# Linear attention times a gated SwiGLU block on one core: a fifth product of the last stage goes to a second Strassen level, and its preparation is moved between engines

## The chip, the cores and the metric

The kernel runs on one core of a Trainium2 chip. The metric is the device time of one execution in microseconds (us); the time before is the median of three runs. PE is the matrix engine TensorE, DVE is VectorE, ACT is ScalarE, POOL is GpSimd, and SP is SyncE, which only issues transfers here. Each engine works through its own queue of instructions in order, and waits at one until the semaphores that it names have come.

## The reference, cut to what matters

```python
xn  = layernorm(x)                       # x: [1, 2048, 1024] bf16
s   = linear_attention(xn, wqkv, wo)     # 32 heads of 32
g   = silu((silu(xn @ w_gate) * (xn @ w_up)) @ w_down)   # F = 3584
out = x + s * g
```

The change touches the product with `w_down` for the second half of the tokens, what prepares its weights, and the loads of `x` and `s` for the last line.

## The kernel before

The 2048 tokens are handled in two passes of 1024. A pass has a gate/up stage (28 weight groups, the products at line 966) that leaves `h`, transposed, in SBUF, and a down stage that multiplies `h` by `w_down`. All large products use the seven-product Strassen-Winograd scheme instead of eight. The first pass ends in `emit_down`, the second in `emit_down_m`.

**The first down stage** (`emit_down`). It goes over token tiles t of 128 in two phases: phase a (four products per k) for tiles 0, 1, then 2, 3; phase b (three products per k) for tiles 2, 3 (`hf == 1`) and then 0, 1 (`hf == 0`). The two tiles of a half are staggered by `LEAD` = 6 of the 14 steps `st`. The sums `dzw` take two of the eight PSUM banks that the pools share out for each tile, and there are two such buffers. So in phase b tile 0 takes over the buffer of tile 2, and tile 1 that of tile 3, once `evac_b` has read them (the VectorE addition `dd`, line 1294, is the first instruction in it on that engine). VectorE, ScalarE and TensorE run in program order here; the `w_down` tiles of phase b are the seven `(p, "b", j)` tiles.

**The second level.** In the last pass seven products M1 to M7 are made one after another, M_ORDER = 1, 2, 7, 6, 5, 4, 3. A product in `L2` is itself split into seven half-width products (`l2_M`, matmuls of 256 columns at line 1466); the others are 56 matmuls of 512 columns (`prod_t`, line 1430). A second-level product needs sums of its weights, four subtractions for each pair j of weight rows, stored to DRAM (`l2_drams`) and loaded again, and sums of its left side (`l2_lhs`). The weight sums come in two ways:

- `l2_early` makes them from the phase b tiles of the first down stage while those lie in SBUF: the subtractions are at line 1132, on GpSimd, and three transfers on SyncE's queue store them (lines 1124 to 1126). The four results T go to the free fourth part of the tile itself. Before, this is done for M2.
- `l2_load` and `l2_sums` load the weights again in the second gate/up stage, into a weight slot, make the sums on GpSimd (line 1144) and store them from its queue (line 1145). Before, this is done for M1 and M4.

**Weight slots.** One pool of eight 1 MB slots (`w_slot`) serves every weight tile. `load_w_to(n)` asks for the tiles up to the n-th of a fixed list `w_seq`; a load waits on SyncE's queue until a slot is free. `r_spare` is a pair of slots that is later used for M1's left-side sums; `x_spare` is a pair of spare tiles for those of M2 and M4.

**The output.** `fin` multiplies by `s` and adds `x` (lines 1200, 1201, VectorE), stores the tile (line 1202), and calls `io_load`, which loads `x` and `s` for a later output tile (lines 1191, 1192, SyncE) into one of five `io` buffers. The last three tiles of the kernel have buffers of their own, in the space of the finished sums S0, S1 and S2:

```python
pool, tg = (sp, "S%d" % len(fq)) if len(fq) < 3 else (iop, "io")
```

In `emit_down_m` the sums kept over the products are KA and KB. M5 gives the block c22 (`tt(c, M5[t], KB[t])`, then silu and `fin`, tile by tile while M5 runs), and M3 is accumulated in PSUM on top of M5 (`out3`, `prod_t(3, t, M5[t], False)`). GpSimd makes M4's left-side sums (lines 1163 to 1166). The functions the diff touches:

Of the kernel before, what the change touches and what calls it, by code (L numbers as in the profile page):

```python
# [10 lines left out]
ALU = mybir.AluOpType  # L11
# [10 lines left out]
def kernel(  # L22
# [165 lines left out]
    passes = list(range(NPASS - 1, -1, -1))  # L188
    NWA = NFG // 2
    M_ORDER = (1, 2, 7, 6, 5, 4, 3)  # L190
    L2 = (1, 2, 4)
    L2_ORDER = (1, 2, 5, 6, 7, 4, 3)
    NQ = NFG // 2
    CH = CW // 2
# [757 lines left out]
    with ExitStack() as p3:  # L952
# [143 lines left out]
            eng.tensor_tensor(out=a21.bitcast(F16), in0=a12, in1=S2, op=ALU.subtract)  # L1096
            s_ring[(hf, m)] = (S1, S2, S3)

        l2_q = deque((M, j) for M in L2 if M != 2 for j in range(0, NQ, 2))
        l2_live = deque()  # L1100

        def l2_load():
            M, j0 = l2_q.popleft()
            kd, q = M_PACK[M]
            t = w_slot()
            v = t[:].rearrange("p h a b -> p (h a b)").rearrange("p (b j n) -> p b j n", b=8, n=CH)
            js = range(j0, min(j0 + 2, NQ))
            for j in js:
                for k, b0, b1 in ((0, 0, 7), (1, 1, 6)):
                    src = wd_drams[j][0 if kd == "a" else 1][:, k, q].rearrange("p (c n) -> p c n", n=CH)  # L1110
                    nc.sync.dma_start(out=v[:, b0:b1 + 1:b1 - b0, j - j0, :], in_=src)
            l2_live.append((M, js, v))

        def l2_early(M, j, store):

            t = w_tiles[(passes[0], "b", j)][:].rearrange("p h a b -> p (h a b)")
            q = M_PACK[M][1]
            w = t[:, 0:6 * CW].rearrange("p (k q c n) -> p q k c n", k=2, q=3, c=2)[:, q]
            T = t[:, 6 * CW:8 * CW].rearrange("p (b n) -> p b n", b=4)
            if store:  # L1120
                if M not in l2_drams:
                    l2_drams[M] = dram.tile([P, 7, NQ, CH], BF16, name="l2_%d" % M)
                d = l2_drams[M]
                nc.sync.dma_start(out=d[:, 0:2, j], in_=w[:, :, 0])
                nc.sync.dma_start(out=d[:, 6, j], in_=w[:, 1, 1])
                nc.sync.dma_start(out=d[:, 2:6, j], in_=T)
                return
            r = w.bitcast(F16) if M >= 4 else w
            t1, t2, t3, t4 = [T[:, i].bitcast(F16) for i in range(4)]
            for o_, a_, b_ in ((t1, r[:, 0, 1], r[:, 0, 0]), (t2, r[:, 1, 1], t1), (t3, r[:, 1, 1], r[:, 0, 1]),  # L1130
                               (t4, r[:, 1, 0], t2)):
                nc.gpsimd.tensor_tensor(out=o_, in0=a_, in1=b_, op=ALU.subtract)

        def l2_sums():
            M, js, v = l2_live.popleft()
# [11 lines left out]
        x_spare, r_spare = [], []  # L1147

        def l2_bufs(M):
            v = [x[:].rearrange("p a b -> p (a b)").bitcast(F16) for x in x_spare]  # L1150
            if M == 1:
                v = [x[:].rearrange("p h a b -> p (h a b)").bitcast(F16) for x in r_spare]
            v = [x[:, 0:2 * NQ * 2 * P].rearrange("p (s j r n) -> p s j r n", s=2, j=NQ, r=2) for x in v]
            return [v[0][:, 0], v[0][:, 1], v[1][:, 0], v[1][:, 1]]

        def l2_quad(A, j):
            v = A[:, :, j].rearrange("p k (r t n) -> p k r t n", r=2, t=2)
            return v[:, 0, :, 0], v[:, 1, :, 0], v[:, 0, :, 1], v[:, 1, :, 1]

        def l2_lhs(M, A, j, eng):  # L1160
            a11, a12, a21, a22 = l2_quad(A, j)
# [22 lines left out]
        def io_load(after=None):  # L1184
            if not fq:
                return
            p, t, cc = key = fq.pop(0)
            r0 = p * TB2 + t * P
            pool, tg = (sp, "S%d" % len(fq)) if len(fq) < 3 else (iop, "io")
            io = pool.tile([P, 2, CW], BF16, name="io", tag=tg)  # L1190
            gate([nc.sync.dma_start(out=io[:, 0, :], in_=x2[r0:r0 + P, cc * CW:(cc + 1) * CW]),
                  nc.sync.dma_start(out=io[:, 1, :], in_=s_dram[r0:r0 + P, cc * CW:(cc + 1) * CW])],
                 after, sync=True)
            io_tiles[key] = io

# [10 lines left out]
        def emit_down(p, h, base, last, more_S, next_S):  # L1206
# [152 lines left out]
            for hf in (1, 0):  # L1359
                t0, t1 = 2 * hf, 2 * hf + 1  # L1360
                fresh = hf == 0
                endz = last and fresh
                for st in range(NFG if endz else NS):
                    if st == 4:
                        while pend:
                            pend.pop(0)()
                    if hf == 1 and not last and st % 2 == 1 and 2 in L2:
                        if st // 2 < NQ:
                            l2_early(2, st // 2, False)
                        if 0 <= st // 2 - 2 < NQ:  # L1370
                            l2_early(2, st // 2 - 2, True)
                    if st < NFG:
                        step_b(t0, st, fresh)
                        if st == NFG - 1:
                            fins = evac_b(t0, fresh)
                    if st >= LEAD and not endz:
                        step_b(t1, st - LEAD, fresh)
                        if fresh and (st - LEAD) % 2 == 1:
                            load_w_to(base + 2 * NWA + (st - LEAD) // 2 + 2)
                if endz:  # L1380
                    for f in fins:
                        f()
                    finish(t1)
                    break
                fins2 = evac_b(t1, fresh)
                for f in fins:
                    f()
                if fresh:
                    deferred.extend(fins2)
                else:  # L1390
                    for f in fins2:
                        f()

        def emit_down_m(p, h, base):
# [8 lines left out]
            def load(M, q=None):  # L1403

                n_ = max(i for i, key in enumerate(seq) if key[2][0] == M and q in (None, key[2][1])) + 1
                load_w_to(base + n_ + (NPK - 2 if M == 1 and q != 3 else NPK))

            def S3(k):
                return s3_[k // NWA][:, k % NWA]
# [59 lines left out]
            def l2_M(M, A, K, done, fill, in_place, dst=None):  # L1469
# [24 lines left out]
                for r in range(2):  # L1494
                    c0, c1 = c[r]
                    if K is None:
                        nc.scalar.copy(out=c1[:, hi], in_=zy[r][:, lo])
                        nc.scalar.copy(out=c0[:, hi], in_=zy[r][:, hi])
                        nc.scalar.copy(out=c0[:, lo], in_=xw[r][:, lo])
                    else:  # L1500
                        tt(c1[:, hi], zy[r][:, lo], K[2 * r + 1][:, hi])
                        tt(K[2 * r][:, hi] if in_place else c0[:, hi], zy[r][:, hi], K[2 * r][:, hi])
# [1 line left out]
                            tt(c0[:, lo], xw[r][:, lo], K[2 * r][:, lo])  # L1504
                    tt(c1[:, hi], xw[r][:, hi], c1[:, hi])
                fill()
                for r in range(2):
                    l2_p(M, 4, r, A, bk)
                load(M, 2)
                for r in range(2):  # L1510
# [2 lines left out]
                        nc.scalar.copy(out=c1[:, lo], in_=zy[r][:, lo])  # L1513
                    else:
                        tt(c1[:, lo], zy[r][:, lo], K[2 * r + 1][:, lo])
                        done(2 * r + 1, c1)
                    l2_p(M, 3, r, A, bk)
                    if in_place:
# [18 lines left out]
            load_w_to(base + NPK - 2)  # L1537
            KA = kept("kA")
            fins = deque()
            M7, M6, M5 = [], [], []  # L1540
            KB = []

            def fill7():
# [17 lines left out]
                flush(1)  # L1561
            load(7)
            sums(S4, A12, S2, ALU.subtract)
            for j in range(NQ):
                l2_lhs(4, quads(h, 1, 1), j, nc.gpsimd)
            M6 = banks()
            for t in range(TPB):
                prod_t(6, t, M6[t], True)
                tt(KB[t], M6[t], KB[t])
                tt(KA[t], M6[t], KA[t])  # L1570
            load(6)
            M5 = banks()
            for t in range(TPB):
                prod_t(5, t, M5[t], True)
                c = k2([P, CW], FP32, "c22")[:]
                tt(c, M5[t], KB[t])
                fins.append((t + TPB, 1, silu(c, "g22")))
                if len(fins) > 1:
                    flush(1)
            tt(KA[-1], M5[-1], KA[-1])  # L1580
            load(5)

            def out3(t):
                prod_t(3, t, M5[t], False)
                c = k2([P, CW], FP32, "c12")[:]
                tt(c, M5[t], KA[t])
                fins.append((t, 1, silu(c, "g12")))

            def done4(t, c):
                fins.append((t + TPB, 0, silu(c, "g21")))  # L1590

            def fill3():
# [21 lines left out]
        for pi, p in enumerate(passes):  # L1614
# [69 lines left out]

            na0 = 6 if first else 8
            l2_j = 0
            load_w_to(base + na0)
            if first:
                wd_pipe2(-1)
# [3 lines left out]
            for i in range(n):  # L1693
# [38 lines left out]
                if not first:  # L1732
                    if l2_live:
                        l2_sums()
                    if i in (17, 18):
                        r_spare.append(w_slot())
                    if i % 2 == 1 and l2_q:
                        l2_load()
                    if i >= 18 and 4 * l2_j + 4 <= i:
                        l2_lhs(1, quads(h, 0, 0), l2_j, nc.gpsimd)  # L1740
                        l2_lhs(2, quads(h, 1, 0), l2_j, nc.gpsimd)
                        l2_j += 1
                if deferred:
                    deferred.pop(0)()
            base += n
            if last_pass:
                l2_lhs(2, quads(h, 1, 0), NQ - 1, nc.gpsimd)
# [36 lines left out]
```

## Time and profile before

| | |
|---|---|
| median of 3 runs | 755.94 us (755.38 to 756.78) |
| profiled execution: its time, its span | 756.18 us, 754.4 us |
| PE busy, share of the span | 745.8 us, 99% |
| DVE / ACT / POOL busy | 581.4 / 381.1 / 399.8 us |
| granted PE clock, mean | 0.999 |
| second pass: gate/up, products | about 498.5 to 668.9 us, 668.9 us to the end |

The page of a profile gives busy times by engine, a chain of work that ended last, and groups of instructions by line. The trace behind it can be asked for the instructions of one engine in order of time: start, duration, engine, line, and in brackets how long the engine stood still just before and what ended that. "SPq" is SyncE's queue, and its lines are the issues of transfers; a transfer "lands" when its data is there. PE is at work for 99% of the span, so a moment in which it stands still is a moment of the total.

### The profile page before, as it was taken

The page shows a single profiled execution, that of the slowest core. Times are in us where ns is not written, and L with a number is a line of the kernel's source. Part 1 is how long each engine was busy: PE and PEld are TensorE (multiplying, and loading weights), DVE is VectorE, ACT ScalarE, POOL GpSimd, SP SyncE. Part 2 cuts the span into 40 slices and gives each one's busy share as a digit, 9 for nine tenths or more (in the row PEclk, how much of TensorE's full clock was granted, in tenths as well). Part 3 has the DMA queues.
Part 4 walks back from the last instruction along what each step waited for, and adds up shares of the span by engine and source line. Part 5 has one row for each costly group of instructions (what it writes and reads, how often), then busy time and mean ns, then how long its engine had stood idle before and what let it go on. Part 6 is the DMA issues. An engine that isn't in the chain of part 4 may idle for free.

```text
span 754.4 us, 11075 instructions
## 1 busy us (share of the span) xinstructions
PE 745.8 (99%) x3857; PEld 360.8 (48%) x3857; DVE 581.4 (77%) x1040; ACT 381.1 (51%) x545; POOL 399.8 (53%) x500
## 2 busy tenths in 40 slices
PE   8999999999999999999999999999999999999997
PEld 3544444454454444444444444444444444467464
DVE  6687787887697788888889785468776877687966
ACT  5677776889956575656658311132323222232023
POOL 2444799998540266868585021811542569434900
PEclk9999999999999999999999999999999999999999
DMA  9967799879779668878799228789786768479652
GB/s 318 304 146 139 228 332 298 303 158 271 206 190 296 231 214 301 295 279 316 273 323 409 111 65 306 222 295 339 258 306 222 281 206 344 147 258 318 209 161 77
DMA packets 129160, 187.77 MB, mean 249 GB/s; under 512 B 36208, under 2 KB 104176, under 8 KB 119376
## 3 DMA queue, kind: packets, MB, share of 16 engines
q1 hardware_dynamic: 121760, 156.00, 63.9%
q0 software_dynamic: 5904, 28.58, 9.9%
q10 hardware_dynamic: 1440, 2.49, 1.1%
q8 instruction: 30, 0.49, 0.3%
q14 instruction: 26, 0.21, 0.1%
HBM read 119.47 MB, written 60.23 MB: 238 GB/s over the span
## 4 chain that ended last, share of the span: by engine, by line
PE 84%; DMA 7%; POOL 3%; DVE 2%; issue 2%; ACT 1%; SPq 1%; POOLq 0%; DVEq 0%; ACTq 0%
PE zw L966 19%; PE kv_ps L554 15%; PE xb L966 10%; PE q_ps L183 6%; PE dzw L1228 6%; PE dm L1430 6%; PE yb L966 5%; PE dm L1466 4%; PE dx L1228 3%; DMA l<-w_sb 3%; PE fx L816 3%; DMA w_sb<-wd 3%; PE s_ps L774 3%; POOL w_sb L1144 2%; PE dy L1228 2%
## 5 line engine op out<-in xcount | busy, mean ns | idle before, releaser
L966 PEld LDWEIGHTS <-w_sb 128*128 128x128 f16 (+1 forms) x1568 | 152.1, 98 | 183.8 <-DMA w_sb<-pk_u 1.3
L966 PE MATMUL xb<-xnT,w_sb 128*128 128x512 bf16 x448 | 115.0, 379 | 0.0
L554 PE MATMUL kv_ps<-wkv_sb,xnT 128*128 128x512 bf16 x512 | 113.7, 379 | 0.6 <-ACT xnT L543 0.4
L966 PE MATMUL zw<-xnT,w_sb 128*128 128x512 bf16 x448 | 105.8, 379 | 0.0
L966 PE MATMUL zw<-S,w_sb 128*128 128x512 f16 x448 | 105.8, 379 | 0.0
L321 POOL TENSOR_TENSOR w_sb<-w_sb 128x512 f16<-128x512 bf16 x42 | 50.2, 1195 | 95.7 <-DVE w_sb L309 51.3
L286 ACT ACTIVATE w_sb<-w_sb 128x2048 bf16<-128x2048 bf16 x42 | 79.9, 1902 | 3.9 <-DMA w_sb<-in_B_w_up_dram 3.9
L554 PEld LDWEIGHTS <-xnT 128*128 128x128 bf16 x512 | 48.3, 97 | 56.0 <-ACT xnT L543 0.8
L1144 POOL TENSOR_TENSOR w_sb<-w_sb 128x512 f16<-128x512 bf16 (+3 forms) x32 | 35.4, 1126 | 52.4 <-DMA w_sb<-wd 51.9
L1042 ACT ACTIVATE sg<-cg 128x1024 bf16<-128x1024 f32 x28 | 29.6, 1057 | 57.4 <-DVE cg L1035 57.4
L183 PE MATMUL q_ps<-xnT,wq_sb 128*128 128x512 bf16 x256 | 58.4, 379 | 0.0
L966 PE MATMUL yb<-S,w_sb 128*128 128x512 f16 x224 | 57.4, 379 | 0.8 <-DMA w_sb<-pk_u 0.8
L1035 DVE SCALAR_TENSOR_TENSOR cg<-zw,rc_all,s 128x1024 f32<-128x1024 f32 x28 | 35.9, 1284 | 25.3 <-PE zw L966 13.2
L994 DVE SCALAR_TENSOR_TENSOR s<-yb,rc_all,s 128x512 f32<-128x512 f32 x42 | 31.5, 749 | 27.3 <-ACT s L993 27.3
L322 POOL TENSOR_TENSOR w_sb<-w_sb 128x512 f16<-128x512 bf16 x42 | 50.5, 1202 | 3.3
L324 POOL TENSOR_TENSOR w_sb<-w_sb 128x512 f16<-128x512 bf16 x42 | 50.3, 1197 | 0.0
L323 POOL TENSOR_TENSOR w_sb<-w_sb 128x512 f16<-128x512 bf16 x42 | 50.2, 1196 | 0.0
L1202 POOL DMA_DIRECT2D out_dram<-io x16 | 8.9, 555 | 69.2 <-DVE io L1201 69.0
L993 ACT ACTIVATE s<-xb,rcl 128x512 f32<-128x512 f32 x14 | 9.6, 687 | 66.3 <-PE xb L966 66.3
L1228 PE MATMUL dx<-w_sb,hT 128*128 128x512 bf16 x112 | 42.4, 379 | 0.0
L993 ACT ACTIVATE s<-xb,rc_all 128x512 f32<-128x512 f32 x42 | 28.4, 676 | 22.0 <-issue 12.7
L309 DVE TENSOR_SCALAR w_sb<-w_sb,cs_all 128x2048 bf16<-128x2048 bf16 x35 | 36.7, 1048 | 2.8
(213 smaller groups left out, 1351.1 us busy)
## 6 DMA issues: line engine op xcount, KB each, us to landing
w_sb<-pk_g SPq DMA_DIRECT2D x27, 1024.0 KB, 6.6
pk_g<-w_sb SPq DMA_DIRECT2D x14, 1024.0 KB, 5.0
w_sb<-pk_u SPq DMA_DIRECT2D x14, 1024.0 KB, 8.3
pk_u<-w_sb POOLq DMA_DIRECT2D x13, 1024.0 KB, 5.8
w_sb<-l SPq DMA_DIRECT2D x9, 896.0 KB, 4.6
w_sb<-in_B_w_gate_dram SPq DMA_DIRECT2D x14, 512.0 KB, 6.4
w_sb<-in_B_w_down_dram SPq DMA_DIRECT2D x28, 256.0 KB, 4.8
w_sb<-in_B_w_up_dram SPq DMA_DIRECT2D x14, 512.0 KB, 5.4
```

Of the source, the lines that this page charges most:

```text
L183: nc.tensor.matmul(q_ps[:], lhsT=wq_sb[:, dc, g * P:(g + 1) * P], rhs=xn_ap(dc, btok), start=(dc == 0), stop=(dc == DC - 1))
L286: nc.scalar.activation(out=junk, in_=raw_view(key, t), func=ACT.Square, accum_out=asum[:])
L321: nc.gpsimd.tensor_tensor(out=T1, in0=b12, in1=b11, op=ALU.subtract)
L322: nc.gpsimd.tensor_tensor(out=T2, in0=b22, in1=T1, op=ALU.subtract)
L323: nc.gpsimd.tensor_tensor(out=T3, in0=b22, in1=b12, op=ALU.subtract)
L324: nc.gpsimd.tensor_tensor(out=T4, in0=b21, in1=T2, op=ALU.subtract)
L554: mm = nc.tensor.matmul(kv_ps[:], lhsT=xn_ap(dc, tok), rhs=wkv_sb[:, dc, c * CW:(c + 1) * CW], start=(dc == 0), stop=(dc == DC - 1))
L966: mm = nc.tensor.matmul(out, lhsT=lhs(k), rhs=rhs(k), start=(first and k == 0), stop=(k == HK - 1), skip_group_check=True)
L993: nc.scalar.activation(out=s1[:], in_=x_[:], func=ACT.Copy, scale=rc)
L1144: nc.gpsimd.tensor_tensor(out=b(o_), in0=b(a_), in1=b(b_), op=ALU.subtract)
L1228: nc.tensor.matmul(out, lhsT=lhs, rhs=rhs, start=first, stop=lastk, skip_group_check=True)
L1430: nc.tensor.matmul(out, lhsT=lhs_of(M)(k)[:, t * P:(t + 1) * P], rhs=w_of(M, k)[:, cols], start=first and k == 0, stop=k == NFG - 1, skip_ ...
```

## The change

- `L2` becomes (1, 2, 4, 5): M5 is made of seven half-width products. Its result is collected in a new tile pair `T5`, in the space S0, S1; `done5` then adds it to KA and KB. c22 is finished (`silu`, `fin`) only in `fill3`, inside M4. M3 starts fresh in its own banks. The first two half products of M4 are made inside M5, as those of M2 are inside M1.
- The weight sums of M2 **and M4** are now made in `l2_early`, on VectorE, in phase b of the first down stage: M2's for tile j at step st = 3 + j, M4's at st = 10 + j, all in `hf == 1`; their stores three and two steps later on SyncE's queue.
- In the second gate/up stage M1 and M5 are loaded again, through two slots that are held for it (`r_spare`) from i = 3 until M5 is done; the prefetch in the last stage is two tiles shorter for that. GpSimd's left-side sums of M2 are spread from i = 4 on.
- The left-side sums of M5 and M4 are made on VectorE by `l2_lhs_all`, eight larger instructions each.
- All residual tiles go through the five `io` buffers. SyncE's queue is in program order in the second gate/up stage.

```diff
-    L2 = (1, 2, 4)
+    L2 = (1, 2, 4, 5)
+    L2_EARLY = (2, 4)
...
         def l2_load():
...
-            t = w_slot()
+            while len(r_spare) < 2:
+                r_spare.append(w_slot())
+            t = r_spare[len(l2_q) % 2]
...
-                nc.gpsimd.tensor_tensor(out=o_, in0=a_, in1=b_, op=ALU.subtract)
+                nc.vector.tensor_tensor(out=o_, in0=a_, in1=b_, op=ALU.subtract)
...
+        def l2_lhs_all(M, A, eng):
+            sb = l2_bufs(M)
+            for r in range(2):
+                v = A.rearrange("p k j (r t n) -> p k j r t n", r=2, t=2)[:, :, :, r]
+                a11, a12, a21, a22 = v[:, 0, :, 0], v[:, 1, :, 0], v[:, 0, :, 1], v[:, 1, :, 1]
+                s1, s2, s3, s4 = [x[:, :, r] for x in sb]
+                eng.tensor_tensor(out=s1, in0=a21, in1=a22, op=ALU.add)
+                eng.tensor_tensor(out=s2, in0=s1, in1=a11, op=ALU.subtract)
+                eng.tensor_tensor(out=s3, in0=a11, in1=a21, op=ALU.subtract)
+                eng.tensor_tensor(out=s4, in0=a12, in1=s2, op=ALU.subtract)
...
         def io_load(after=None):
-            pool, tg = (sp, "S%d" % len(fq)) if len(fq) < 3 else (iop, "io")
+            pool, tg = iop, "io"
...
         def emit_down(p, h, base, last, more_S, next_S):
-                    if hf == 1 and not last and st % 2 == 1 and 2 in L2:
-                        if st // 2 < NQ:
-                            l2_early(2, st // 2, False)
-                        if 0 <= st // 2 - 2 < NQ:
-                            l2_early(2, st // 2 - 2, True)
+                    if not last:
+                        for M, q0, dq, lag in zip(L2_EARLY, (3, 10), (1, 1), (3, 2)):
+                            for d, store in ((0, False), (lag, True)):
+                                j, rem = divmod(st + (1 - hf) * NS - q0 - d, dq)
+                                if rem == 0 and 0 <= j < NQ:
+                                    l2_early(M, j, store)
...
         def emit_down_m(p, h, base):
-                load_w_to(base + n_ + (NPK - 2 if M == 1 and q != 3 else NPK))
+                load_w_to(base + n_ + (NPK - 2 if M in (1, 2, 7, 6, 5) and (M, q) != (5, 3) else NPK))
...
-            for j in range(NQ):
-                l2_lhs(4, quads(h, 1, 1), j, nc.gpsimd)
+            l2_lhs_all(5, quads(h, 0, 1).bitcast(F16), nc.vector)
...
-            M5 = banks()
-            for t in range(TPB):
-                prod_t(5, t, M5[t], True)
-                c = k2([P, CW], FP32, "c22")[:]
-                tt(c, M5[t], KB[t])
-                fins.append((t + TPB, 1, silu(c, "g22")))
-                if len(fins) > 1:
-                    flush(1)
-            tt(KA[-1], M5[-1], KA[-1])
-            load(5)
+            l2_lhs_all(4, quads(h, 1, 1), nc.vector)
+            T5 = [sp.tile([P, 2, CW], FP32, name="kT", tag="S%d" % r) for r in range(2)]
+            T5 = [T5[t // 2][:, t % 2] for t in range(TPB)]
...
+            def done5(t, T):
+                tt(KA[t], T, KA[t])
+                tt(T, T, KB[t])
...
             def fill3():
+                for t in range(TPB):
+                    fins.append((t + TPB, 1, silu(T5[t], "g22")))
                 flush()
+                M3.extend(banks())
                 out3(0)
-            go(l2_M(4, quads(h, 1, 1), KB, done4, fill3, True))
+            m4_ = l2_M(4, quads(h, 1, 1), KB, done4, fill3, True)
+            go(l2_M(5, quads(h, 0, 1).bitcast(F16), None, done5, lambda: next(m4_), False, T5))
+            go(m4_)
...
+            if last_pass:
+                sp_man.enter_context(tc.manual_schedule(engines={mybir.EngineType.SP}))
...
-                    if i in (17, 18):
-                        r_spare.append(w_slot())
-                    if i % 2 == 1 and l2_q:
+                    if i >= 3 and i % 2 == 1 and l2_q:
                         l2_load()
```

More of the change, by code (lines that the diff above doesn't have):

```diff
@@ L1097, in emit_hs @@
             s_ring[(hf, m)] = (S1, S2, S3)
-        l2_q = deque((M, j) for M in L2 if M != 2 for j in range(0, NQ, 2))
+        l2_q = deque((M, j) for M in L2 if M not in L2_EARLY for j in range(0, NQ, 2))
         l2_live = deque()
+        x_spare, r_spare = [], []
         def l2_load():
@@ L1145, in l2_sums @@
             nc.gpsimd.dma_start(out=l2_drams[M][:, :, js.start:js.stop, :], in_=v[:, 0:7, 0:n_, :])
-        x_spare, r_spare = [], []
         def l2_bufs(M):
             v = [x[:].rearrange("p a b -> p (a b)").bitcast(F16) for x in x_spare]
-            if M == 1:
+            if M in (1, 5):
                 v = [x[:].rearrange("p h a b -> p (h a b)").bitcast(F16) for x in r_spare]
@@ L1188, in io_load @@
             r0 = p * TB2 + t * P
-            pool, tg = (sp, "S%d" % len(fq)) if len(fq) < 3 else (iop, "io")
+            pool, tg = iop, "io"
             io = pool.tile([P, 2, CW], BF16, name="io", tag=tg)
-            gate([nc.sync.dma_start(out=io[:, 0, :], in_=x2[r0:r0 + P, cc * CW:(cc + 1) * CW]),
-                  nc.sync.dma_start(out=io[:, 1, :], in_=s_dram[r0:r0 + P, cc * CW:(cc + 1) * CW])],
+            eng = nc.sync
+            gate([eng.dma_start(out=io[:, 0, :], in_=x2[r0:r0 + P, cc * CW:(cc + 1) * CW]),
+                  eng.dma_start(out=io[:, 1, :], in_=s_dram[r0:r0 + P, cc * CW:(cc + 1) * CW])],
                  after, sync=True)
@@ L1497, in l2_M @@
                         nc.scalar.copy(out=c1[:, hi], in_=zy[r][:, lo])
-                        nc.scalar.copy(out=c0[:, hi], in_=zy[r][:, hi])
-                        nc.scalar.copy(out=c0[:, lo], in_=xw[r][:, lo])
                     else:
@@ L1506, in l2_M @@
                 fill()
+                if K is None:
+                    for r in range(2):
+                        nc.scalar.copy(out=c[r][0][:, hi], in_=zy[r][:, hi])
+                        nc.scalar.copy(out=c[r][0][:, lo], in_=xw[r][:, lo])
                 for r in range(2):
@@ L1515, in l2_M @@
                         tt(c1[:, lo], zy[r][:, lo], K[2 * r + 1][:, lo])
+                    if done is not None:
                         done(2 * r + 1, c1)
@@ L1539, in emit_down_m @@
             fins = deque()
-            M7, M6, M5 = [], [], []
+            M7 = []
             KB = []
@@ L1571, in emit_down_m @@
             load(6)
-            M5 = banks()
-            for t in range(TPB):
-                prod_t(5, t, M5[t], True)
-                c = k2([P, CW], FP32, "c22")[:]
-                tt(c, M5[t], KB[t])
-                fins.append((t + TPB, 1, silu(c, "g22")))
-                if len(fins) > 1:
-                    flush(1)
-            tt(KA[-1], M5[-1], KA[-1])
-            load(5)
+            l2_lhs_all(4, quads(h, 1, 1), nc.vector)
+            T5 = [sp.tile([P, 2, CW], FP32, name="kT", tag="S%d" % r) for r in range(2)]
+            T5 = [T5[t // 2][:, t % 2] for t in range(TPB)]
             def out3(t):
-                prod_t(3, t, M5[t], False)
+                prod_t(3, t, M3[t], True)
                 c = k2([P, CW], FP32, "c12")[:]
-                tt(c, M5[t], KA[t])
+                tt(c, M3[t], KA[t])
                 fins.append((t, 1, silu(c, "g12")))
@@ L1590, in done4 @@
                 fins.append((t + TPB, 0, silu(c, "g21")))
+            def done5(t, T):
+                tt(KA[t], T, KA[t])
+                tt(T, T, KB[t])
+            M3 = []
             def fill3():
+                for t in range(TPB):
+                    fins.append((t + TPB, 1, silu(T5[t], "g22")))
                 flush()
+                M3.extend(banks())
                 out3(0)
-            go(l2_M(4, quads(h, 1, 1), KB, done4, fill3, True))
+            m4_ = l2_M(4, quads(h, 1, 1), KB, done4, fill3, True)
+            go(l2_M(5, quads(h, 0, 1).bitcast(F16), None, done5, lambda: next(m4_), False, T5))
+            go(m4_)
             hs_ = [slice(0, 3 * CW // 4), slice(3 * CW // 4, CW)]
@@ L1686 @@
             l2_j = 0
+            sp_man = ExitStack()
+            if last_pass:
+                sp_man.enter_context(tc.manual_schedule(engines={mybir.EngineType.SP}))
             load_w_to(base + na0)
@@ L1734 @@
                         l2_sums()
-                    if i in (17, 18):
-                        r_spare.append(w_slot())
-                    if i % 2 == 1 and l2_q:
+                    if i >= 3 and i % 2 == 1 and l2_q:
                         l2_load()
-                    if i >= 18 and 4 * l2_j + 4 <= i:
+                    if i >= 19 and 4 * l2_j + 4 <= i:
                         l2_lhs(1, quads(h, 0, 0), l2_j, nc.gpsimd)
-                        l2_lhs(2, quads(h, 1, 0), l2_j, nc.gpsimd)
                         l2_j += 1
+                    if i % 4 == 0 and i >= 4:
+                        l2_lhs(2, quads(h, 1, 0), i // 4 - 1, nc.gpsimd)
                 if deferred:
                     deferred.pop(0)()
+            sp_man.close()
             base += n
```

## The prediction, made before the changed kernel had run

> **What bounds the kernel now.** The page first: TensorE works in 99% of the span, so it is the bound in every stage.
>
> ```profile
> PE 745.8 (99%) x3857; PEld 360.8 (48%) x3857; DVE 581.4 (77%) x1040; ACT 381.1 (51%) x545; POOL 399.8 (53%) x500
> ```
>
> A change can win in two ways only: fewer matmuls, or less of the few microseconds in which TensorE stands still. It loses wherever it makes TensorE wait. The chain that ended last gives the pace of the two kinds of product, and TensorE's timeline the two waits that the changed places hold today:
>
> ```profile
> 734.62 3.02 PE dm L1430 x14
> 737.64 3.06 PE dm L1466 x28
> 623.81 1.04 PE L966 MATMUL yb<-S,w_sb 128*128 128x512 f16 x4 [0.82 <-DMA w_sb<-pk_u]
> 728.35 1.69 PE L1466 MATMUL dm<-w_sb,hT 128*128 128x256 f16 x14 [0.28 <-ACT dm L1478]
> ```
>
> A 512-column matmul takes 3.02 / 14 = 0.2157 us, a 256-column one 3.06 / 28 = 0.1093 us. Next, what VectorE does when the first down stage changes from tiles 2, 3 to tiles 0, 1 (timelines of VectorE, then of TensorE):
>
> ```profile
> 448.97 0.42 DVE L1093 TENSOR_TENSOR S<-hT 128x512 f16<-128x512 bf16 x1
> 449.42 0.42 DVE L1094 TENSOR_TENSOR S<-S,hT 128x512 f16<-128x512 f16 x1
> 449.76 0.42 DVE L1095 TENSOR_TENSOR S<-hT 128x512 f16<-128x512 bf16 x1
> 450.22 0.42 DVE L1096 TENSOR_TENSOR hT<-hT,S 128x512 f16<-128x512 bf16 x1
> ...
> 468.10 1.23 DVE L714 TENSOR_TENSOR xnT<-xnT,S 128x2048 f16<-128x2048 bf16 x1
> 469.24 0.42 DVE L1200 TENSOR_TENSOR g<-g,io 128x512 bf16<-128x512 bf16 x1
> ...
> 476.05 1.22 DVE L1294 TENSOR_TENSOR dd<-dzw,s 128x1024 f32<-128x1024 f32 x1 [5.14 <-PE dzw L1228]
> 480.58 1.23 DVE L1294 TENSOR_TENSOR dd<-dzw,s 128x1024 f32<-128x1024 f32 x1 [3.31 <-PE dzw L1228]
> ```
> ```profile
> 480.60 0.59 PE L1228 MATMUL dzw<-w_sb,hT 128*128 128x512 f16 x2
> ...
> 484.48 0.59 PE L1228 MATMUL dzw<-w_sb,hT 128*128 128x512 f16 x2
> ```
>
> VectorE stands idle 5.14 us before the first `dd` (tile 2) and 3.31 us before the second (tile 3). TensorE takes those two buffers again at 480.60 and 484.48, so the first `dd`, over at 477.3, has 3.3 us to spare. Last, the tail on VectorE and SyncE:
>
> ```profile
> 750.75 0.35 DVE L1200 TENSOR_TENSOR g<-g,io 128x384 bf16<-128x384 bf16 x1
> 751.13 0.36 DVE L1201 TENSOR_TENSOR io<-g,io 128x384 bf16<-128x384 bf16 x1
> 751.41 0.22 DVE L1200 TENSOR_TENSOR g<-g,io 128x128 bf16<-128x128 bf16 x1
> ```
> ```profile
> 736.86 0.34 SPq L1202 DMA_DIRECT2D out_dram<-io  x1
> 738.58 0.33 SPq L1191 DMA_DIRECT2D io<-in_A_x_dram  x1
> 738.96 1.00 SPq L1192 DMA_DIRECT2D io<-s_dram  x1
> ```
>
> A residual load waits until the store from its buffer has landed: here 1.7 us, in other pairs of this stretch up to 2.6.
>
> **Part 1, the weight sums on VectorE.** GpSimd loses 28 subtractions of 0.705 us (19 us); VectorE gets 56 of 128x256. The trace has no such two-byte row on VectorE; the sizes around it are 128x128 (0.22 us) and 128x384 (0.35), so I take 0.285. Starts lie the duration plus 0.03 apart where one needs the result before it, and the duration less 0.07 where not (0.45 and 0.34 for the 0.42 us rows above). Four for one pair j make 2 x 0.315 + 2 x 0.21 = 1.05 us.
>
> In the changed kernel's instruction order, eleven of the fourteen groups (M2's seven, M4's first four) stand **ahead of** the first `dd`, and three between it and the second. Ahead of them is the same work as before, to 469.24, and two `fin` (1.58 us). So the first `dd` starts at 469.24 + 1.58 + 11 x 1.05 = 482.4 and ends at 483.6: TensorE waits 3.0 us. The second ends at 483.6 + 3 x 1.05 + 1.22 = 488.0; TensorE, now 3.0 late, wants it at 487.5: 0.5 more. **Cost 3.5 us**; nothing hides it, as TensorE has no gap before the end. If the sums ran at the 128x128 rows (0.80 a group), the cost would be 0.2; at the 128x384 rows (1.32), 7.2. The true size lies midway, so I keep 3.5 and both ends for the range.
>
> M4's sums overwrite the T area of M2's, so each also waits for M2's store on SyncE. The stores stand behind the first gate tile's load, which landed at 475.8 before; its tiles can be asked for earlier now, as SyncE no longer waits 25.6 us for GpSimd's first sums. Uncovered, this adds up to 2 us. Behind the stores are 10 residual loads and the load of the first up tile, issued at 494.32 before and wanted about 7.5 us later; I get 496.3, against a TensorE that is 3.5 us late. Cost nothing, by about 2 us.
>
> The granted clock was 1.00 throughout the down stage and 0.91 only in the last 10.4 us, where TensorE idled 4.6. The Trainium skill ("TensorE: Matmul & The Clock Gate", Part 1) says that an idle window of some 3.4 us halves the clock until TensorE has again been busy for as long. By it a 3.0 us wait is just spared, and a longer one could cost some 1.7 us more, an estimate from that page.
>
> **Part 2, M5.** It goes from 56 x 0.2157 = 12.08 us to 98 x 0.1093 = 10.71: **1.4 us gained**, and the 0.28 wait at M4's start goes too, as ScalarE no longer has a c22 silu in front of that copy. VectorE gets 16 left-side sums of 896 columns (about 0.6 each, between the 512 and 2048 rows above: 9.5 us) and some 3.7 us more of additions, but GpSimd's 28 sums (29 us) leave, beside which VectorE's 128x1024 sums took 1.06 instead of some 0.7. I get M6's additions done by 718, and M4 takes those banks at 722. Cost nothing; with that 4 us cover gone, microsecond for microsecond.
>
> The prefetch is two tiles shorter in M1 and M2: M7's first tile is asked for at 679.4 (when M2's first tile is free) instead of 675.4, and is wanted from 687.1 on; it landed in 5.5. Cost nothing, up to 1.5.
>
> **Part 3, the second gate/up stage.** SyncE's queue waited 47 us for stores of the slots that the sums passed through; with two slots of their own the 0.82 us wait should go: **0.8 gained**. Next late would be the sums themselves (load, sums, store: about 19 us of a 24 us cycle). A loss of the same size bounds it on the other side.
>
> **Part 4, the residual tiles.** Four c22 `fin`, formerly 3 us apart within M5, now come together when M4's fifth half product is done (732.7): VectorE ends them at 734.8, 735.6, 736.4, 737.2. SyncE's order is then store, store, store, load, load, load, store, load (each load a pair), each load behind the landing of an earlier store (1.9 us): the fourth store goes out at 739.5, its load at 741.4, and it lands (2.3 us) at 744.1. That tile is for the first `fin` after M3's second tile, where VectorE would be at 742.5. The last three tiles have lost their own buffers and come behind the stores of that same run: the last lands at 751.5, and the final `fin` ends at 752.6 instead of 751.9. So the end is 0.7 later, although TensorE ends 1.7 earlier. With landings of 2.6 us it is 1.7 later, without any wait 1.7 earlier. I take **1.2 later, M5's gain used up in it**.
>
> **The sum**: 3.5 - 0.8 + 1.2 = 3.9. The profiled execution took 756.18 us (span 754.4); 756.18 + 3.9 = 760.1. It lay 0.24 above the median, so 759.8.
>
> **The rivals.** (a) *Faster*: the sums cost VectorE little enough that the buffer is free in time. The first `dd` must end by 480.6, so eleven groups have 8.55 us, 0.78 each; and the tail must not wait. Then 755.9 - 0.8 - 1.7 = 753.4. For: VectorE is idle for 8.4 us there. Against: even the half-size row gives 0.80. (b) *Only the stall*: the residual tiles come in time; 755.9 + 3.5 - 0.8 - 1.7 = 756.9. For: stores can land in 1.7. Against: SyncE's order of stores and loads. (c) *Heavier*: M4's sums wait for the stores, the clock drops or M7's weights are late; 2 to 5 us on top, 762 to 765. For: the first gate tile took 12.9 us to land. Against: less is queued beside it now.
>
> **How the numbers follow.** About 0.2% (1.5 us) can be told from no change. Forecast 0.50, heavier 0.24, both slower; (b) 0.12, counted as the same; (a) 0.14. The range reaches from 755.0, below (b) and above (a), to 764.5, the upper end of the sums plus a late tail.
>
> **What would show it.** TensorE idle about 3 us ahead of the `dzw` matmul of tile 0 at 480.6, released by VectorE's `dd`, which comes after eleven groups of some 1.05 us; no idle time before the first of the two `dd`; no wait near 620; M5 with 98 matmuls of 0.109; VectorE waiting for an `io` load between 742 and 751 of the old time. The prediction is wrong if `dd` still starts at 476, or if TensorE takes other banks first.

## The result and the profile after

The changed kernel takes 762.54 us (median of 9 runs) against 756.65 us of the kernel before on the same chip: ratio 1.0073, interval 1.0057 to 1.0089, so slower, as forecast: 5.9 us more by these medians, where 3.9 more were forecast (759.8, range 755.0 to 764.5, from a median before of 755.94). The profiled execution took 762.54 us, its span is 760.8 us, 6.4 more than before. The page's busy times:

```profile
PE 741.0 (97%) x3835; PEld 365.0 (48%) x3899; DVE 592.1 (78%) x1119; ACT 385.2 (51%) x557; POOL 356.4 (47%) x444
```

TensorE's share fell from 99% to 97%: what was lost, it lost standing still. (Some 64 of its matmuls are missing from this record, so its busy time is a little low; it has 42 more to do than before, 98 of M5 for 56.) Its timeline shows two waits, in the first down stage and just behind it:

```profile
482.94 0.59 PE L1242 MATMUL dzw<-w_sb,hT 128*128 128x512 f16 x2 [1.79 <-DVE dd L1308]
...
512.08 1.04 PE L967 MATMUL yb<-S,w_sb 128*128 128x512 f16 x4 [1.54 <-DMA w_sb<-pk_g]
```

The first was forecast, at 3.0 + 0.5 us. VectorE's timeline (line 1136 are the weight sums, 1308 is the `dd`) shows why it is shorter, and a later wait of VectorE for a residual load, at 496.74:

```profile
472.33 9.41 DVE L1136 TENSOR_TENSOR w_sb<-w_sb 128x256 f16<-128x256 bf16 x40
481.66 1.22 DVE L1308 TENSOR_TENSOR dd<-dzw,s 128x1024 f32<-128x1024 f32 x1
482.80 2.88 DVE L1136 TENSOR_TENSOR w_sb<-w_sb 128x256 f16<-128x256 f16 x12
485.59 1.22 DVE L1308 TENSOR_TENSOR dd<-dzw,s 128x1024 f32<-128x1024 f32 x1
...
496.74 0.43 DVE L1214 TENSOR_TENSOR g<-g,io 128x512 bf16<-128x512 bf16 x1 [5.95 <-DMA io<-s_dram]
```

Ten groups pass in 9.33 us, 0.93 each; VectorE does not stand still before `dd`, and the second `dd` is in time. The wait at 496.74 is not new, but in the kernel before it ended 3.8 us earlier:

```profile
492.98 0.42 DVE L1200 TENSOR_TENSOR g<-g,io 128x512 bf16<-128x512 bf16 x1 [5.10 <-DMA io<-s_dram]
```

The second wait of TensorE, for a gate tile, was not in the sum. SyncE's timeline shows what stood ahead of that tile:

```profile
490.75 0.83 SPq L1130 DMA_DIRECT2D l<-w_sb  x1
491.69 0.67 SPq L1205 DMA_DIRECT2D io<-in_A_x_dram  x1
...
497.88 0.38 SPq L264 DMA_DIRECT2D w_sb<-pk_u  x1
504.48 0.33 SPq L1205 DMA_DIRECT2D io<-in_A_x_dram  x1
...
505.40 0.39 SPq L264 DMA_DIRECT2D w_sb<-pk_g  x1
```

and in the kernel before:

```profile
488.33 0.35 SPq L1191 DMA_DIRECT2D io<-in_A_x_dram  x1
...
494.32 0.38 SPq L263 DMA_DIRECT2D w_sb<-pk_u  x1
...
499.83 0.38 SPq L263 DMA_DIRECT2D w_sb<-pk_g  x1
```

The gate tile stands behind one residual load, which waits until an output tile has left its buffer: VectorE's `fin` at 496.74, its store from GpSimd's queue at 497.92, landed at 504.4, 6.5 us later. Before, the same store took from 494.16 to 498.9. So the gate tile is asked for 5.6 us later than before, while TensorE is only 2.3 us later. Of the 5.6, 3.8 come from the later `fin`, whose own residual load went out at 491.69 instead of 488.33 (SyncE comes to it straight from the last of M4's stores; but the output tile whose buffer it takes was itself stored only at 487.89 instead of 485.50); the other 1.8 come from the slower landing of the store. The table by stretches of 5 us shows what else is new there (columns: stretch, length, busy time of PE, PEld, DVE, ACT and POOL with counts, granted clock, busy share of the DMA engines, GB/s). Two stretches of the kernel before:

```profile
485.00:490.00 5.00, 5.00 (x25) 2.27 (x24) 2.78 (x7) 0.00 (x0) 3.21 (x6) 1.00 0.60 184
495.00:500.00 5.00, 5.00 (x25) 2.23 (x23) 2.29 (x4) 1.76 (x2) 0.00 (x0) 1.00 0.77 265
```

and the same of the changed kernel:

```profile
485.00:490.00 5.00, 4.95 (x24) 2.25 (x23) 4.86 (x13) 1.15 (x1) 1.60 (x3) 1.00 1.00 279
495.00:500.00 5.00, 5.00 (x25) 2.27 (x24) 2.58 (x4) 1.21 (x2) 0.54 (x1) 1.00 1.00 254
```

With M4's 3 MB of stores the DMA engines are full from 475 to 500. Last, the tail, on VectorE and on SyncE:

```profile
748.28 0.43 DVE L1214 TENSOR_TENSOR g<-g,io 128x512 bf16<-128x512 bf16 x1 [2.51 <-DMA io<-s_dram]
...
753.92 0.43 DVE L1214 TENSOR_TENSOR g<-g,io 128x512 bf16<-128x512 bf16 x1 [0.97 <-DMA io<-s_dram]
```
```profile
738.57 1.92 SPq L1216 DMA_DIRECT2D out_dram<-io  x3
...
743.41 0.42 SPq L1216 DMA_DIRECT2D out_dram<-io  x1
745.72 0.33 SPq L1205 DMA_DIRECT2D io<-in_A_x_dram  x1
```

TensorE's last matmul ends at 751.05; VectorE's last `fin` at 757.85, 6.8 us behind it. Before it was 2.1 (749.80 and 751.89).

**The 6.4 us, read from the two traces**: 0.57 had passed before the changed place (I don't count it to the change: in the other runs' profiles VectorE reached the same instruction there 0.8 us earlier to 0.6 us later than before); + 1.79 for `dd`; + 1.54 for the gate tile; − 0.82, the wait near 620, which is gone; − 1.82 from M6's first matmul to M3's second tile (38.33 us before, 36.51 after); + 4.71, the tail of VectorE behind TensorE; + 0.4 behind the last `fin`.

### The profile page after: what moved, and what is told of

Same layout as the page of the kernel before. It is cut to its first block, busy times and chain, and to the rows that moved or that the text cites. A ratio compares the mean times of both kernels' runs of the same rounds, so it can differ in the third digit from the quotient of the medians.

```text
span 760.8 us, 11165 instructions
## 1 busy us (share of the span) xinstructions
PE 741.0 (97%) x3835; PEld 365.0 (48%) x3899; DVE 592.1 (78%) x1119; ACT 385.2 (51%) x557; POOL 356.4 (47%) x444
## 4 chain that ended last, share of the span: by engine, by line
PE 88%; DVE 5%; DMA 4%; issue 1%; ACT 1%; SPq 0%; DVEq 0%; ACTq 0%
PE zw L967 25%; PE kv_ps L555 14%; PE xb L967 12%; PE q_ps L183 6%; PE yb L967 6%; PE dzw L1242 5%; PE dm L1481 4%; PE dm L1445 3%; PE fx L817 3%; PE s_ps L775 2%; PE dx L1242 2%; PE dy L1242 2%; DVE w_sb L1136 1%; PE kvz L577 1%; PE nd L744 1%
## 5 line engine op out<-in xcount | busy, mean ns | idle before, releaser
L967 PE MATMUL xb<-xnT,w_sb 128*128 128x512 bf16 x420 | 113.3, 379 | 1.5
```

The costliest lines, as they stand in the source:

```text
L967: mm = nc.tensor.matmul(out, lhsT=lhs(k), rhs=rhs(k), start=(first and k == 0), stop=(k == HK - 1), skip_group_check=True)
```

## Experiments

All were compared with the kernel before on their own chip. One thousandth in a ratio is 0.76 us. The changed kernel stands at 1.0073.

**The buffers of the last tiles.** Edit:

```diff
-            pool, tg = iop, "io"
+            pool, tg = (sp, "S%d" % len(fq)) if len(fq) < 3 else (iop, "io")
...
-            T5 = [sp.tile([P, 2, CW], FP32, name="kT", tag="S%d" % r) for r in range(2)]
-            T5 = [T5[t // 2][:, t % 2] for t in range(TPB)]
+            T5 = xnp.tile([P, TPB, CW], FP32, name="kT", tag="xn8")
+            T5 = [T5[:, t] for t in range(TPB)]
```

> The changed kernel with one thing undone: the last three residual tiles have buffers of their own again (M5's T tiles take another tile instead). Theory A (the tail is late because those tiles wait for the stores of the same run): the waits of 2.5, 1.0 and 0.8 us on VectorE after 748 go, the last fin ends some 2.1 us after TensorE's last matmul as it did in the kernel before, instead of 6.8: 4.7 us less, 757.8. Rival B (the tail is late because the four c22 fin come together and the stores with them, whatever buffers the last tiles have): the waits stay, 762.5 within 1 us.

Measured: 761.21 us, ratio 1.0039 (1.0023 to 1.0056). The waits behind 752 are gone, but VectorE still waits 3.02 us at 748.8, and its last `fin` ends 5.2 us behind TensorE. By the ratios it is 2.6 us less than the changed kernel, where theory A had 4.7. So both theories were half right: the buffers are 1.6 of the 4.7 us of the tail in the profile, and something else is 3.1.

The same cause alone, in the kernel before (only the first pair of lines above, the other way round):

> The kernel before with that one thing alone: all residual tiles pass through the five io buffers. Theory A (the buffers are enough to make the tail late): 3 to 5 us slower than before, 759.5 to 761.5. Rival B (it takes the bunched c22 fin as well, here they lie 3 us apart): at most 1 us slower, 756.5 to 757.5.

Measured: 759.32 us, ratio 1.0017 (0.9999 to 1.0036), between the two and just not clear of no change. In the profile the last `fin` ends 4.3 us behind TensorE, 2.2 more than before: the buffers cost about that on their own, without any bunching.

**The order in which the tiles are loaded.** The first `fin` after M3's second tile is that of c12's first tile; in the list of loads this tile stands behind the four of c21, so it is the fourth of the loads that follow the c22 stores. Edit, with own buffers:

```diff
-                fq += [(p, t + dt, cc) for dt, cc in ((0, 0), (TPB, 1), (TPB, 0), (0, 1)) for t in range(TPB)]
+                fq += [(p, t + dt, cc) for dt, cc in ((0, 0), (TPB, 1)) for t in range(TPB)]
+                fq += [(p, 0, 1)] + [(p, t + TPB, 0) for t in range(TPB)] + [(p, t, 1) for t in range(1, TPB)]
```

> The changed kernel with own buffers for the last three residual tiles, and with the residual loads of the last pass in the order in which the fin take them (the first c12 tile ahead of the four c21 tiles instead of behind them). Theory A (VectorE's wait of 2.5 to 3.0 us at 748 arises because the first fin after M3's second tile takes the tile that was asked for last): that tile is asked for long before, the wait shrinks to the 0.5 us or less that the last of the four loads is late for its own fin, and the last fin ends some 2.1 us after TensorE: 2.5 less than with own buffers alone, 758.5 against 761.2. Rival B (the wait is passed on to the next fin, whose loads are as late): less than 1 us, 760.5 or more.

Measured: 758.96 us, ratio 1.0012 (1.0001 to 1.0023). Theory A. VectorE's timeline has one wait for a transfer left in the tail:

```profile
747.99 0.43 DVE L1215 TENSOR_TENSOR g<-g,io 128x512 bf16<-128x512 bf16 x1 [0.51 <-DMA io<-s_dram]
```

The last `fin` ends 2.7 us behind TensorE. SyncE's queue is what it was (the fourth store at 742.7, its load at 745.2): that load is as late as ever, but now it belongs to the fourth `fin` after M3's second tile, not to the first.

This run's profile also shows, unasked, what a slightly longer wait does:

```profile
482.32 0.89 PE L1243 MATMUL dzw<-w_sb,hT 128*128 128x512 f16 x2 [2.23 <-DVE dd L1309]
483.00 0.63 PE L1243 MATMUL dx<-w_sb,hT 128*128 128x512 bf16 x1
```

A `dx` matmul is shown with 0.63 instead of 0.38, and the granted clock of 480 to 485 is 0.75. Three groups of three matmuls (two `dzw`, one `dx`) take 3.63 us, from 482.32 to 485.95, instead of 1.94: 1.7 us on top of the wait.

**The work ahead of `dd`.** The four 128x2048 sums of the next pass stand ahead of the weight sums on VectorE (4.9 us). Edit:

```diff
             if not last:
                 emit_rcl()
-                emit_Ssum(passes[passes.index(p) + 1])
...
                 fins2 = evac_b(t1, fresh)
+                if not last and not fresh:
+                    emit_Ssum(passes[passes.index(p) + 1])
```

> The changed kernel with the four 128x2048 sums of the next pass (4.9 us on VectorE) moved behind the last of the down stage's dd. Theory A (the first dd is late because of the work queued ahead of it on VectorE, and the gate tile is late because SyncE's queue waits for the weight sums): the 1.8 us wait before the dzw product goes, M4's stores are over some 4 us earlier and so is the gate tile: both waits gone, 3.3 us less, 759.2. Rival B (SyncE is paced by its own 21 stores, not by the sums): the first wait goes and the gate tile, no earlier than before, makes TensorE wait 3.3 us instead of 1.5: 762.5, no change. A second rival: M4's sums wait for M2's stores to land, and the first wait stays too.

Measured: 761.13 us, ratio 1.0039 (1.0024 to 1.0054): 2.6 less than the changed kernel, where 3.3 were expected. The `dd` wait is all but gone and so is that for the gate tile, but part is given back (TensorE's timeline):

```profile
485.79 0.59 PE L1242 MATMUL dzw<-w_sb,hT 128*128 128x512 f16 x2 [0.15 <-DVE dd L1308]
...
502.11 1.89 PE L967 MATMUL zw<-S,w_sb 128*128 128x512 f16 x8 [1.05 <-DVE dd L1302]
```

Two more waits for VectorE follow, 0.81 us at 509.12 and 0.67 us at 531.57. The moved sums now delay the `fin`, hence their stores, hence the next residual load; VectorE waits 5.53 us for it at 500.0 with the next `dd` queued behind it. (The profiled execution, 762.34 us, was 1.2 above the median.)

**Part 1 alone**, in the kernel before (the early sums of M2 and M4 on VectorE with their stores; all else as before):

> The kernel before with part 1 alone: the early sums of M2 and M4 on VectorE, with their stores, as in the changed kernel; M5, the staging, the prefetch and the residual tiles as before. Theory A (part 1's cost is two waits of its own, which nothing else in the change brings about): 1.8 us before the dzw product and 1.5 us for the gate tile appear, the 0.8 us near 620 goes, the tail is as before: 756.7 + 2.5 = 759.2. Rival B (the waits come from the other parts too, such as the residual buffers): one of them is missing, 757.5 or less.

Measured: 759.50 us, ratio 1.0027 (1.0014 to 1.0039). Theory A in the main, with a third wait: TensorE waits 1.82 us before `dzw`, 1.47 us before the first up tile's product and 0.74 us before the next gate tile's; the wait near 620 is gone, and the last `fin` ends 2.1 us behind TensorE. (For the 1.47 us the profile names a VectorE addition that ended just then; but in the changed kernel the same product begins 0.85 us before that addition does, and the weight load of this product, which begins with it at 505.82, is shown waiting for the up tile.) In the run with own buffers it is 1.62 us for the up tile and 0.26 for the gate tile. So the late weight tiles belong to part 1; which of them is late differs. The wait near 620 is gone here without the two slots held for the reloads; but here M1 alone is loaded again.

**Queue or transfer?** First, M4's stores to another queue:

```diff
-                nc.sync.dma_start(out=d[:, 0:2, j], in_=w[:, :, 0])
+                e = nc.sync if M == 2 else nc.gpsimd
+                e.dma_start(out=d[:, 0:2, j], in_=w[:, :, 0])
...
```

> The changed kernel with M4's 21 stores of weight sums on GpSimd's queue instead of SyncE's. Theory A (the gate tile is 5.6 us later than before because SyncE's stores of M4's sums stand ahead of the residual loads): the residual loads go out at about 484 instead of 492, VectorE's wait of 5.95 us for one of them goes or shrinks to 1, the gate tile is asked for before 501 and TensorE's wait of 1.5 us goes: 761.0. Rival B (the gate tile hangs on VectorE's fin behind the late dd, or on the landing of loads beside the stores): the wait stays, 762.5. The wait before the dzw product, 1.8 us, stays in both.

Measured: 765.78 us, ratio 1.0106 (1.0080 to 1.0131): 2.5 slower than the changed kernel, which neither theory had. GpSimd's queue holds the stores of the output tiles, and these now stand behind M4's. Its timeline, and VectorE's:

```profile
498.87 0.54 POOL L1217 DMA_DIRECT2D out_dram<-io  x1 [4.94 <-DMA l<-w_sb]
```
```profile
504.47 0.42 DVE L1215 TENSOR_TENSOR g<-g,io 128x512 bf16<-128x512 bf16 x1 [13.53 <-DMA io<-s_dram]
```

The residual loads go out at 501.7 instead of 492, and TensorE waits 4.04 us for a `dd` behind that `fin`, with a slow stretch after it.

Second, the same bytes in longer runs (for M2 and M4, loads and the use at the products accordingly):

```diff
-                    l2_drams[M] = dram.tile([P, 7, NQ, CH], BF16, name="l2_%d" % M)
+                    l2_drams[M] = dram.tile([P, NQ, 7, CH], BF16, name="l2_%d" % M)
...
-                nc.sync.dma_start(out=d[:, 2:6, j], in_=T)
+                nc.sync.dma_start(out=d[:, j, 2:6], in_=T)
```

> The changed kernel with the early sums of M2 and M4 stored pair by pair: the array in memory has the order [partition, j, product, column] instead of [partition, product, j, column], so that the stores write runs of 1 and 2 KB instead of 512 bytes, and the loads of M2's and M4's tiles read runs of 1 KB instead of 3.5. Number and order of all instructions stay. Theory A (the gate tile is late because the DMA engines are full: busy 0.98 to 1.01 of the time from 475 to 500, against 0.60 to 0.77 before): the stores are done and the residual loads land earlier, VectorE's wait of 5.95 us for one shrinks to 4 or less, and TensorE's wait of 1.5 us for the gate tile goes: 1.5 less, 761.0. Rival B (only the order in SyncE's queue counts, in which nothing changes): the wait stays, no change within 0.5. In both the wait of 1.8 us before the dzw product stays. A loss of 1 to 2 us is possible if M2's or M4's tiles now land late.

Measured: 760.82 us, ratio 1.0037 (1.0024 to 1.0050), 2.7 us less than the changed kernel by the ratios; with the two intervals the expected 1.5 is as possible. TensorE's only wait left is the 1.79 us for `dd`. In the stretches of 5 us:

```profile
485.00:490.00 5.00, 5.00 (x25) 2.29 (x24) 4.83 (x11) 1.15 (x1) 2.09 (x4) 1.00 0.89 291
495.00:500.00 5.00, 5.00 (x25) 2.27 (x24) 2.58 (x4) 1.76 (x2) 0.54 (x1) 1.00 0.70 218
```

From 470 to 500 there are 7,382 packets instead of 13,303 for about the same 8.3 MB, and 330 to 336 GB/s instead of 280 to 284 while the engines are full (475 to 485). The store ahead of the gate tile lands 4.7 us after its issue instead of 6.5, and the tile is asked for at 502.34 instead of 505.40 (this profile was 0.75 us earlier already ahead of the change). One point missed: VectorE's wait for the residual load shrinks only to 5.56 us, so its `fin` is nearly as late as in the changed kernel. So the 1.8 us that the full DMA engines added to the landing of that store decided whether the gate tile came in time: the order in the queue did not change. The later `fin` is the larger share of its delay, and by itself it cost TensorE nothing here.

**Put together.** First own buffers, the c22 stores on ScalarE's queue, the sums moved as above, and the long runs:

> All four together: own residual buffers, c22 stores on ScalarE, the next pass's sums behind the last dd, and the long rows in the stores. Theory (the waits are separate and none is given back): the 1.8 and 1.5 us waits of TensorE and the 4.5 us of the tail go: 762.5 - 7.8 = 754.7, ratio to before 0.997. Rival (the 5.5 us wait of VectorE for a residual load moves on to the next dd, as when the sums alone were moved): TensorE waits about 1 us at 502, 756, ratio 0.999.

Measured: 756.83 us, ratio 0.9996 (0.9982 to 1.0010): the rival. (What the c22 stores on ScalarE's queue give alone was not measured.) TensorE waits 0.8 and 1.4 us behind VectorE's late `fin`, and VectorE 1.16 us in the tail. Next the moved sums went behind the first three `fin` of six, and the loads into the order of use:

> All together: own residual buffers, residual loads in the order of use, c22 stores on ScalarE, long rows in the stores, and the next pass's sums behind the last dd and behind three of the six fin that follow it, so that their stores and the next residual load come earlier than in the version with all four. Theory (what was given back there, 0.8 + 1.4 us behind the fin that waits for a residual load, and 1.2 us in the tail, goes with it): 756.8 - 3.4 = 753.5, ratio to before 0.9955. Rival (the wait for the residual load is a matter of full DMA engines and stays, or the up tile now comes late): 755.5 to 757.

Measured: 756.05 us, ratio 0.9982 (0.9968 to 0.9995). The tail is as short as before (2.1 us), and those two waits are gone, but the first up tile now stands behind residual loads that wait for landings:

```profile
504.60 1.04 PE L973 MATMUL yb<-S,w_sb 128*128 128x512 f16 x4 [2.06 <-DMA w_sb<-pk_u]
505.48 1.83 PE L973 MATMUL xb<-xnT,w_sb 128*128 128x512 bf16 x4
```

The four `xb` matmuls and the eight `zw` after them take 1.7 us more than elsewhere (1.83 against 1.03, 2.81 against 1.89). Last, five of those residual loads went to ScalarE's queue:

```diff
-            eng = nc.sync
+            eng = io_eng.popleft() if io_eng else nc.sync
...
+                if not last and not fresh:
+                    io_eng.extend([nc.scalar] * 5)
                 for f in fins:
                     f()
```

> The version with all in order, and the five residual loads that follow the fin of the first down stage on ScalarE's queue, which has nothing to do from 485 to 496, instead of SyncE's. Theory A (there TensorE's wait of 2.06 us for the first up tile, and the halved clock after it, some 1.7 us, came from that tile standing behind residual loads on SyncE, which wait for stores to land): the up tile is asked for at about 491 instead of 497.6 and the wait and the slow stretch go; nothing else is late, so of the kernel before M5's 1.6 us and the 0.8 us near 620 are gained: 753.5 to 754, ratio 0.996. Rival B (the full DMA engines set when the up tile lands, or the second gate tile is late next): a wait of 1 to 2 us stays, 755.5 to 757.

Measured: 754.73 us, ratio 0.9968 (0.9955 to 0.9980): faster than both kernels. The up tile is asked for at 493.96; one wait is left, and it keeps the full clock:

```profile
506.70 1.89 PE L973 MATMUL zw<-xnT,w_sb 128*128 128x512 bf16 x8 [1.27 <-DVE s L1015]
```

VectorE is late there because a `fin` waited 2.36 us for a residual load. With it gone the time would be some 1.3 us lower still, an estimate from that wait; no run shows it.

## Why the prediction was right, step by step

- **The stall at `dd`: right in place and kind, 1.79 instead of 3.5 us.** Eleven groups, then `dd`, then three groups, as laid out. The term that was mis-sized is the group: 0.93 us, not 1.05. The 0.285 us of one subtraction was exact (285 ns in the trace); the spacing was not: eleven times 0.12 us is the 1.3 us by which the first `dd` came earlier than forecast, counted from where TensorE stood. The last 0.5 of the 3.5, a second wait, did not come: the second `dd` ends 3.93 us behind the first (forecast 4.37), and TensorE wants its buffer 3.88 us after the first.
- **"Cost nothing, by about 2 us" for the weight tiles: wrong.** I counted SyncE's queue only, and only as far as the up tile. That tile went out at 497.9 (forecast 496.3) and was in time; the gate tile behind it was not, 1.54 us. The `fin` whose store it stood behind was 3.8 us later; but the experiment with long runs shows that another term, which the sum did not have, decided it: the landing of that store, 1.8 us slower while the DMA engines were full. Rival (c) had a loss by the stores, but by another path, M4's sums waiting for them. Moving M4's stores to GpSimd's queue, as a count of SyncE's queue would suggest, made it worse.
- **M5: right**, 1.82 with its wait, forecast 1.7. VectorE's cover held: nothing of TensorE waits there.
- **Second gate/up stage: right**, 0.82. SyncE's waits for the stores of the sums' slots fell from 47.0 to 20.8 us, and the gap in its weight loads from 609.99 to 618.67, behind which the late up tile went out, is gone: from 596.88 to 639.19 one goes out about every 6.05 us. That the two slots did it is not shown by a run: with part 1 alone, without them but with fewer reloads, the wait was gone too.
- **The tail: right in mechanism, mis-sized**: 5.1 us with what follows the last `fin`, forecast 2.9. The term is when the c22 `fin` end: forecast 734.8 to 737.2, which with TensorE's 1.3 us would be 736.1; the first ended at 738.5. VectorE's queue of M5's additions and M4's (line 1433) runs without a break from 729.4, and the `fin` stand behind it. I also named SyncE's order and the own buffers as the whole cause; the run with the loads in the order of use shows that the list, which the change did not touch, decides which `fin` has to wait for the late load.
- **The sum** was 3.9; the traces give 6.4 less the 0.57 from ahead of the change, 5.8. The errors are −1.7 (`dd`), +1.5 (gate tile) and +2.1 (tail with M5: 3.3 instead of 1.2), so the near miss owes something to errors of both signs.
- **The clock rule** did not come into play in the changed kernel (1.00 after 1.79 us). My use of it, that 3.0 us would be just spared, does not hold: 2.06 us were not spared in one run, see the last section.

## What to carry to other kernels

Work that moves off an idle engine takes its transfers along: look at the busy share of the DMA engines in the stretch where they land, and at what the freed or refilled buffers release, not only at the queue that issues them. Where buffers are recycled by store, landing and load, the loads belong in the order of use, and on a queue where nothing urgent stands behind them. Here most removals gave part of their gain back to the next instruction in an in-order queue; only with the whole chain in order did the time fall under that of before.

## What the runs showed of the hardware

- **A wait of 2 us can halve the clock.** After 2.06 and 2.23 us without a matmul the granted clock fell (0.66 and 0.75 over 5 us; behind the second wait matmuls of 512 columns start 0.43 us apart instead of 0.216), and TensorE lost another 1.7 us each time; after 1.79, 1.82 and, in one run, 2.20 us it stayed at 1.00. The Trainium skill ("TensorE: Matmul & The Clock Gate", Part 1) gives an idle window of some 3.4 us; it also says that the window runs free. That this lets waits of about the same length fall on either side, as 2.06, 2.20 and 2.23 us did, is my reading and is not shown. The measured 2.06 us is below its figure, and the cost after it near the 1.7 us that I had estimated.
- **Runs of 512 bytes are not enough for the full rate here.** With the early sums stored in runs of 512 bytes, the stretches from 475 to 485 moved 280 to 284 GB/s; with the same bytes in runs of 1 and 2 KB, 330 to 336; the busy share was 0.95 to 1.01 in both, and other transfers ran beside them in both. The Trainium skill ("DMA: Bandwidth & Descriptors", Specifications) puts the least size for the line rate at 512 bytes; here the rate still rose by 16 to 20% above it; where the runs lie in memory changed with their length.
